# Fourth-quarter rows in a dead transform buffer, phase products in the spectrum buffers, and forward steps early in the inverse stage

## Chip, cores and metric

The kernel runs on one core of a Trainium2 chip. The metric is the device time of one execution in microseconds (us), median of several runs.

## The reference, cut to what matters

```python
# x: 8 x 5696 x 128 (batch, sequence, channels), h: 5696 x 128
Xf = np.fft.rfft(x, n=2 * S, axis=1); Hf = np.fft.rfft(h, n=2 * S, axis=0)
x  = np.fft.irfft(Xf * Hf[None], n=2 * S, axis=1)[:, :S]      # long convolution

theta = x @ w_theta                                            # 128 x 128
zr, zi = x * np.cos(theta), x * np.sin(theta)                  # the "phases"
y = einsum('ts,bsd->btd', w_tok_r, zr) + einsum('ts,bsd->btd', w_tok_i, zi)   # 5696 x 5696, twice
u = x + y
return u + np.maximum(u @ w_ch, 0.0)
```

## The kernel before

The kernel has three parts, one after the other.

1. **Block transform.** Eight groups (`bp`, `dh`: a batch pair and half of the channels). A group has forward steps A (tile `a`), spectrum steps B (products `u_t`, `v_t` of the spectrum with `hs`, which is loaded in chunks of 128 KB), inverse steps C (tile `g`) and output steps D (tile `yt`, stored to `yt_hbm`). C of one group is woven with A of the next; then B of the next is woven with D of this one. Stretches are named after the round of this loop: the "spectrum stretch of the seventh group" holds D of the seventh and B of the eighth group.
2. **Rows and phase steps.** The result, transposed by way of HBM, comes back as rows `ya0` and `ya1` (batches 0-3 and 4-7). 44 phase steps follow, 22 for each half: four transposes, a copy `y_ap`, its store, the matmuls of `theta`, three ACT operations (Abs, Sin, Sin), two DVE products, and the store of the products to `z_hbm`. Sixteen steps of the first half are woven into the last group.
3. **Block multiplication** (tiles `m`, `c`): a block scheme over the 5696 x 5696 weights. Its right-hand sides `b` are read back from `z_hbm` and summed ("`b` sums"), its weights `wb` are loaded, transposed and summed on DVE.

```python
fx = pool("fft_x", 1, xin)
fc = pool("fft_c", 1, conv, side="right")
fa = pool("fft_a", 1, conv, side="right")
fs = pool("fft_s", 2, conv, side="right")
fh = pool("fft_h", 4, conv, side="right")          # the hs buffers
...
# stage B, one chunk c
nc.scalar.activation(xs[:, :, :, :ck], ps, AF.Copy)
for r in range(2):
    nc.vector.tensor_tensor(uv[r][:, :, :, c0:c0 + ck], xs[:, :, :, :ck],
                            hv[:, r:r + 1, :, :ck].to_broadcast([P, 2, HD, ck]), op=mult)
load(c + LEAD)                                      # the hs load four chunks on, SP queue
...
# stage C, chunk q = 0, 8, ..., 120: 16 matmuls, then one eviction
if q % 24 == 16:
    nc.scalar.activation(...); nc.scalar.mul(...)   # on ACT
else:
    nc.vector.tensor_tensor(g_out, g_in, sg, op=mult)
...
# the phases
both = sb.tile([P, 2, n], F32, tag="both", name="both")       # pool "s2": 2 buffers
mag, red = both[:, 0, :], both[:, 1, :]
...
nc.scalar.activation(mag, r, AF.Abs)
nc.scalar.activation(red, r, AF.Sin, bias=zero_b[:m], scale=-TWO_PI)
nc.scalar.activation(mag, mag, AF.Sin, bias=half_pi[:m], scale=-TWO_PI)
zi = red.bitcast(BF16)[:, :n]                       # products in place
zr = mag.bitcast(BF16)[:, :n]
zi_eng.tensor_mul(zi, red, yflat)
nc.vector.tensor_mul(zr, mag, yflat)
nc.sync.dma_start(z_hbm[...], both[rows].bitcast(BF16)[:, :, :n])
...
def phase_step(ti, hh):
    ...
    y_ap = st["sby"].tile([P, 4, D], BF16, tag="y", name="y_ap")   # pool "s2y": 2 buffers
    nc.vector.tensor_copy(y_ap, tpz)
    nc.sync.dma_start(y2_hbm[ti]..., y_ap...)
...
for g, (bp, dh) in enumerate(groups):
    ...
    if dh == 0 and bp + 1 < B // 2:
        woven(c_, (a_ + [next_x], 0.7), now, load_)  # next_x loads 2.9 MB
    else:
        woven(c_, a_, now, load_)
    if g + 2 == len(groups):
        load_ya(0)                                  # 2.9 MB, ACT queue
    woven(b_, stage_d(st, bp, dh), now)
...
load_ya(1)                                          # after the last group
for step in steps0:
    step()
```

Of the kernel before, what the change touches and what calls it, by code (L numbers as in the profile page):

```python
# [10 lines left out]
F32 = mybir.dt.float32  # L11
BF16 = mybir.dt.bfloat16
F16 = mybir.dt.float16
# [9 lines left out]
def kernel(  # L23
# [10 lines left out]
    nc = tc.nc  # L34
    B, S, D = x.shape
    assert D == 128
    P = 128
# [29 lines left out]
    H = 22 * P  # L67
# [28 lines left out]
    def psum():  # L96
        return fp.tile([P, 2, 512], F32, tag="ps", name="ps")

    conv, setup, xin, pha = ExitStack(), ExitStack(), ExitStack(), ExitStack()

    def pool(name, bufs, stack, **kw):
        return stack.enter_context(tc.tile_pool(name=name, bufs=bufs, **kw))

    fx = pool("fft_x", 1, xin)
    fc = pool("fft_c", 1, conv, side="right")
    fa = pool("fft_a", 1, conv, side="right")
    fs = pool("fft_s", 2, conv, side="right")
    fh = pool("fft_h", 4, conv, side="right")
    s1 = pool("set_1", 1, setup, side="right")
    s2 = pool("set_2", 2, setup, side="right")  # L110

# [101 lines left out]

    def woven(*lists):

        lists = [l if isinstance(l, tuple) else (l, 1.0) for l in lists]
        steps = [((i + 0.5) / len(l) * w, n, f) for n, (l, w) in enumerate(lists) for i, f in enumerate(l)]
        for _, _, f in sorted(steps, key=lambda s: s[:2]):
            f()

# [88 lines left out]
    def stage_c(st):  # L309
        sg = sgn[:K1].unsqueeze(2).unsqueeze(1).to_broadcast([K1, 2, N2, 8])  # L310

        def chunk(q):
            if q == 0:
                st["g"] = fg.tile([P, 2 * N2, P], F16, tag="g", name="g_")
            ps = psum()
            for i in range(8):
                o = ps[:, i // 4, (i % 4) * P:(i % 4 + 1) * P]
                at = (q + i) * K1
                nc.tensor.matmul(o, u_t[:, at:at + P], r_u, start=True, stop=False)  # L319
                nc.tensor.matmul(o, v_t[:, at:at + P], r_v, start=False, stop=True)  # L320
            g_out = st["g"][:K1, :, q:q + 8].rearrange("p (r n) q -> p r n q", r=2)
            g_in = ps[:K1].rearrange("p a (q r n) -> p r n (a q)", q=4, r=2)
            if q % 24 == 16:
                nc.scalar.activation(g_out[:, :, :EN], g_in[:, :, :EN], AF.Copy)
                nc.scalar.mul(g_out[:, :, EN:], g_in[:, :, EN:], sgn[:K1, EN:EN + 1])
            else:
                nc.vector.tensor_tensor(g_out, g_in, sg, op=mult)
        return [lambda q=q: chunk(q) for q in range(0, 2 * HD, 8)]
# [39 lines left out]
    def phases_b(ti, y_ap, b0, nb, yT, sb, th_pool, th_tag, zi_eng, turns=None, tags=("red", "mag"), m=P,  # L368
# [2 lines left out]
        if theta_ps is None:  # L371
            theta_ps = th_pool.tile([P, n], F32, tag=th_tag, name="theta_ps")
        theta_ps = theta_ps[:m]
        if tags is None:
            both = sb.tile([P, 2, n], F32, tag="both", name="both")
            mag, red = both[:, 0, :], both[:, 1, :]
        else:
            red = sb.tile([P, n], F32, tag=tags[0], name="red")[:m]
            mag = sb.tile([P, n], F32, tag=tags[1], name="mag")[:m]
        y_ap = y_ap[:m]  # L380
        if turns is None:
            for b in range(nb):
# [21 lines left out]
        nc.scalar.activation(red, r, AF.Sin, bias=zero_b[:m], scale=-TWO_PI)  # L404
        nc.scalar.activation(mag, mag, AF.Sin, bias=half_pi[:m], scale=-TWO_PI)
        yflat = y_ap.rearrange("p b d -> p (b d)")
        zi = red.bitcast(BF16)[:, :n]
        zr = mag.bitcast(BF16)[:, :n]
        zi_eng.tensor_mul(zi, red, yflat)  # L409
        nc.vector.tensor_mul(zr, mag, yflat)  # L410
        cols = slice(b0 * D, b0 * D + n)
        for e in range((m + 63) // 64):
            rows = slice(e * 64, e * 64 + 64)
            if ti * P >= 2 * H:
                for r, z in enumerate((zr, zi)):
                    nc.sync.dma_start(zl_hbm[r, :, cols], z)
                continue
            p_, blk = divmod(2 * ti + e, 4 * NJ)
            i, j = divmod(blk, NJ)
            if tags is None:  # L420
                nc.sync.dma_start(z_hbm[:, p_, j, i, :, cols].rearrange("z t n -> t z n"),
                                  both[rows].bitcast(BF16)[:, :, :n])
            else:
                for r, z in enumerate((zr, zi)):
                    nc.sync.dma_start(z_hbm[r, p_, j, i, :, cols], z[rows])
# [20 lines left out]
        nc.scalar.mul(w_neg, w_theta_sb, -1.0)  # L446
        st["turns"] = (ones, plus, minus, w_neg)

    def load_ya(hh):
        st = sides["phases"]  # L450
        ya = st[hh] = pool(f"s2a{hh}", 1, pha, reuse_waits="tile").tile([P, 4, H], BF16, name=f"ya{hh}")
        PW = QR
        for p_ in range(4):
            nc.scalar.dma_start(ya[:, :, p_ * PW:p_ * PW + PW],
                                yt_hbm[:, 4 * hh:4 * hh + 4, p_ * PW:p_ * PW + PW])

    def phase_step(ti, hh):

# [18 lines left out]
    for g, (bp, dh) in enumerate(groups):  # L477
# [5 lines left out]
        if dh == 0 and bp + 1 < B // 2:  # L483
            def next_x(bp=bp):
                x16s[bp + 1] = load_x(bp + 1)
            woven(c_, (a_ + [next_x], 0.7), now, load_)
        else:
            woven(c_, a_, now, load_)
        if g + 2 == len(groups):
            xin.close()  # L490
            open_phases()
            load_ya(0)
        now = [steps0.pop(0) for _ in range(6)] if last else []
        woven(b_, stage_d(st, bp, dh), now)
    conv.close()

    CHUNKS = [(j0, min(CJ, NJ - j0)) for j0 in range(0, NJ, CJ)]
# [26 lines left out]
        nc.vector.tensor_add(b12, b11, b12)  # L524
        nc.vector.tensor_add(b21, b21, b22)  # L525

    load_ya(1)
    for step in steps0:
        step()
    early = iter(range(NE))  # L530
# [4 lines left out]
    for j in early:  # L535
        load_b(0, j, bpe)
    pha.close()
    psp.close()

    tp = ctx.enter_context(tc.tile_pool(name="tpool", bufs=5, reuse_waits="tile"))  # L540
# [354 lines left out]
```

## Time and profile before

The kernel took 2234.97 us (median of 3, 2234.55 to 2238.08; a fourth run, timed with the changed kernel, makes it 2235.14). To see where a change moves time, I cut the span at the first spectrum matmul of a group, the last spectrum matmul (in the round of the seventh group), the first and last output matmul of the last group, the Abs of the 23rd and of the 44th phase step, and the tenth addition to `c` (about the end of the multiplication's first tile pair). Each figure is the difference of the start times of two such instructions in the trace.

| stretch, us | before |
|---|---|
| setup, to the first spectrum matmul | 65.8 |
| transform, to the last spectrum matmul of the seventh group | 351.6 |
| last group's inverse stretch | 39.0 |
| last group's output stretch | 14.2 |
| to the 23rd phase step | 42.6 |
| 21 steps more, to the 44th | 67.2 |
| start of the multiplication | 56.4 |
| the rest | 1598.0 |

The chain of waits of the kernel before shows that the rest is PE at work on the tile `m`, which the change doesn't touch:

```profile
## 4 chain that ended last, share of the span: by engine, by line
PE 61%; DVE 5%; DMA 4%; POOL 2%; issue 1%; ACT 0%; DVEq 0%; ACTq 0%; SPq 0%; POOLq 0%
PE m L834 56%; DMA wb<-in_moe_w_tok_r_dram 2%; POOL wb L556 2%; DVE c L841 2%; DMA wb<-in_moe_w_tok_i_dram 1%; PE utp L646 1%; PE v L653 1%; DVE wt L565 1%; PE m L795 1%; PE m L797 1%; PE m L838 1%; PE tpz L595 0%; PE theta_ps L383 0%; DMA b<-z_hbm 0%; DVE b L525 0%
```

Next, the busy times of the engines by stretch, of the kernel before. The first number after the stretch is its length, and the last three are the granted clock of PE, the DMA share and GB/s. The rows are a set of inverse and forward steps, the spectrum and output steps after it, the coming of the second half of the rows, and the 22 steps of that half.

```profile
core 0: us, PE busy (x) PEld busy (x) DVE busy (x) ACT busy (x) POOL busy (x), PEclk, DMA share, GB/s
88.20:112.60 24.40, 24.37 (x316) 24.09 (x316) 12.63 (x11) 16.03 (x25) 4.23 (x8) 0.88 0.27 58
112.60:138.10 25.50, 17.17 (x491) 15.45 (x489) 15.81 (x25) 17.15 (x20) 4.19 (x8) 0.80 0.87 195
...
473.00:499.00 26.00, 10.63 (x66) 6.69 (x65) 7.14 (x13) 7.14 (x12) 11.52 (x22) 0.57 1.16 265
499.00:579.00 80.00, 48.21 (x326) 32.44 (x327) 52.54 (x92) 42.56 (x73) 0.00 (x0) 0.63 0.71 198
```

In the inverse and forward steps PE is busy all the time. In the spectrum and output steps no engine is: PE waits a third of it. In the phase steps no engine is busy for over two thirds of 80 us. The reasons stand in two lists of waits, again of the kernel before. First, what PE waited for before the first of the two inverse matmuls:

```profile
L319 PE MATMUL ps<-r_u,u_t x1024: 216/219/314, 88.2 to 454.3; 128*128 128x128 f16 x171
its engine sat idle before it (us, times) until:
  DVE u_t L303: 25.5, 8
```

PE stands still about 3 us at each of eight changes from spectrum to inverse steps, until the last products `u_t` are there. Second, the waits of the phase steps, from 440 to 580 us (engine, what it was about to do, what it waited for: us in all, times, longest):

```profile
ACT both L403 <- DMA z_hbm<-both: 38.2, 17, 4.6
...
PE ps L394 <- DVE y_ap L466: 20.4, 17, 2.6
...
ACT both L403 <- DMA ya<-yt_hbm: 9.3, 1, 9.3
...
DVE y_ap L466 <- DMA y_hbm<-y_ap: 5.0, 2, 3.6
```

ACT waits 38 us for stores of `both`: there are two such tiles, and ACT may not write a tile again before its products have landed in HBM.

### The profile page before, as it was taken

Reading aid. Unit: us, or ns where it says so; the run is one execution under the profiler, and the core shown is the slowest. Engines: PE = TensorE matmul, PEld = TensorE weight load, DVE = VectorE, ACT = ScalarE, POOL = GpSimd, SP = SyncE. Lnnn points to the kernel's source line nnn. Section 1 sums busy time; section 2 is a strip of 40 time slices with the busy share of each in tenths; the row PEclk is TensorE's granted clock in tenths of the full one; section 3 lists DMA queues with packets and bytes.
Section 4 is the critical chain, followed back from the end, with each engine's and each line's share of the span. In section 5 each row is a group of like instructions: output and inputs, shape, how many; then the busy total and the mean of one; then the engine's idle time right before and its main releaser. Section 6 shows DMA issues by size and latency. Waiting matters only on the chain.

```text
span 2234.9 us, 41331 instructions
## 1 busy us (share of the span) xinstructions
PE 2025.2 (91%) x15679; PEld 1134.5 (51%) x15679; DVE 1630.4 (73%) x2972; ACT 667.5 (30%) x1000; POOL 856.4 (38%) x1568
## 2 busy tenths in 40 slices
PE   3788888656699999999999997899999999999997
PEld 3777888644344444444444443344444444444443
DVE  7756656646798888877876766967777776867773
ACT  5767767655333232323320000011111111111111
POOL 4301010020145454455366552354444535454440
PEclk8688889876799999999999999899999999999998
DMA  7356463587899998989899989597878879797872
GB/s 142 78 129 161 123 158 85 157 208 209 235 172 171 174 177 167 173 143 171 163 191 149 152 128 279 101 154 135 153 135 139 148 130 154 129 159 128 152 130 53
DMA packets 410649, 340.39 MB, mean 152 GB/s; under 512 B 83288, under 2 KB 365784, under 8 KB 409336
## 3 DMA queue, kind: packets, MB, share of 16 engines
q0 software_dynamic: 221312, 143.00, 47.7%
q1 hardware_dynamic: 182032, 179.41, 27.9%
q10 hardware_dynamic: 7104, 15.34, 1.9%
q8 instruction: 123, 2.02, 0.4%
q14 instruction: 78, 0.63, 0.1%
HBM read 382.55 MB, written 97.93 MB: 215 GB/s over the span
## 4 chain that ended last, share of the span: by engine, by line
PE 61%; DVE 5%; DMA 4%; POOL 2%; issue 1%; ACT 0%; DVEq 0%; ACTq 0%; SPq 0%; POOLq 0%
PE m L834 56%; DMA wb<-in_moe_w_tok_r_dram 2%; POOL wb L556 2%; DVE c L841 2%; DMA wb<-in_moe_w_tok_i_dram 1%; PE utp L646 1%; PE v L653 1%; DVE wt L565 1%; PE m L795 1%; PE m L797 1%; PE m L838 1%; PE tpz L595 0%; PE theta_ps L383 0%; DMA b<-z_hbm 0%; DVE b L525 0%
## 5 line engine op out<-in xcount | busy, mean ns | idle before, releaser
L556 POOL DMA_DIRECT2D wb<-in_moe_w_tok_i_dram x720 | 387.8, 546 | 801.3 <-DVE wt L565 719.2
L556 POOL DMA_DIRECT2D wb<-in_moe_w_tok_r_dram x720 | 386.9, 548 | 283.4 <-ACT both L404 166.9
L834 PE MATMUL m<-b,wt 128*128 128x512 bf16 x1936 | 454.0, 382 | 22.2 <-DVE wt L565 21.2
L565 DVE STREAM_TRANSPOSE wt<-wb 128x384 f32<-128x384 f32 (+2 forms) x720 | 359.9, 524 | 124.5 <-PE m L834 69.2
L834 PEld LDWEIGHTS <-wt 128*128 128x128 bf16 x1936 | 189.7, 98 | 256.0 <-DVE wt L565 24.3
L841 DVE TENSOR_TENSOR c<-c,m 128x512 f32<-128x512 f32 x440 | 284.0, 671 | 0.0
L648 ACT ACTIVATE uts<-utp 128x512 bf16<-128x512 bf16 (+1 forms) x90 | 53.3, 593 | 616.1 <-PE utp L646 616.1
L319 PE MATMUL ps<-r_u,u_t 128*128 128x128 f16 x1024 | 139.9, 230 | 30.5 <-DVE u_t L303 25.5
L320 PE MATMUL ps<-r_v,v_t 128*128 128x128 f16 x1024 | 138.6, 230 | 0.0
L643 ACT ACTIVATE ub<-c 128x512 bf16<-128x512 f32 (+1 forms) x90 | 56.5, 628 | 227.5 <-DVE c L841 227.2
L319 PEld LDWEIGHTS <-u_t 128*128 128x128 f16 x1024 | 108.6, 106 | 26.9 <-DVE u_t L303 26.9
L127 POOL DMA_DIRECT2D x<-in_x_dram x64 | 34.1, 538 | 206.0 <-PE ps L190 195.9
L320 PEld LDWEIGHTS <-v_t 128*128 128x128 f16 x1024 | 106.6, 104 | 6.4 <-issue 5.7
L303 DVE TENSOR_TENSOR u_t<-xs,hs 128x1024 f16<-128x1024 f16 x96 | 64.9, 676 | 53.9 <-ACT xs L301 31.4
L301 ACT ACTIVATE xs<-ps 128x1024 f16<-128x1024 f32 x96 | 92.6, 990 | 21.9 <-PE ps L208 10.2
L208 PEld LDWEIGHTS <-w_t 64*128 64x128 f16 x3240 | 67.3, 106 | 52.8 <-issue 37.3
L190 PE MATMUL ps<-f_t,x 89*128 89x180 f16 x512 | 87.4, 308 | 3.5 <-ACT xs L301 2.3
L597 ACT ACTIVATE yb<-tpz 128x512 bf16<-128x512 bf16 (+1 forms) x46 | 27.5, 597 | 166.6 <-PE tpz L595 137.3
L190 PEld LDWEIGHTS <-x 89*128 89x128 f16 x512 | 74.4, 239 | 4.2 <-issue 3.9
L385 ACT ACTIVATE red<-theta_ps,magic 128x512 f32<-128x512 f32 (+1 forms) x46 | 31.6, 687 | 140.9 <-PE theta_ps L383 124.8
L655 DVE SCALAR_TENSOR_TENSOR c<-v,c 128x512 f32<-128x512 f32 (+1 forms) x90 | 61.5, 684 | 11.1 <-PE v L653 8.6
L409 DVE TENSOR_TENSOR both<-both,y_ap 128x512 bf16<-128x512 f32 x44 | 30.3, 689 | 48.6 <-ACT both L404 48.4
(2847 smaller groups left out, 3835.7 us busy)
## 6 DMA issues: line engine op xcount, KB each, us to landing
wb<-in_moe_w_tok_r_dram POOLq DMA_DIRECT2D x352, 96.0 KB, 4.7
wb<-in_moe_w_tok_i_dram POOLq DMA_DIRECT2D x352, 96.0 KB, 4.8
wb<-in_moe_w_tok_r_dram POOLq DMA_DIRECT2D x352, 80.0 KB, 4.5
wb<-in_moe_w_tok_i_dram POOLq DMA_DIRECT2D x352, 80.0 KB, 3.9
hs<-hf_hbm SPq DMA_DIRECT2D x192, 128.0 KB, 3.5
cp_hbm<-c SPq DMA_DIRECT2D x88, 256.0 KB, 2.2
c<-cp_hbm SPq DMA_DIRECT2D x88, 256.0 KB, 4.5
out_dram<-c SPq DMA_DIRECT2D x88, 256.0 KB, 4.4
```

Source lines behind the costliest of these rows:

```text
L190: nc.tensor.matmul(ps[:, i // 2, (i % 2) * 2 * K1:(i % 2 + 1) * 2 * K1], lhs(q + i), f1_t[:NB], start=True, stop=True)
L208: nc.tensor.matmul(ps[:, e, j * HD:(j + 1) * HD], w_t2[rows, c0 + j, N2 * (1 - ri):N2 * (3 - ri)], a_st["a"][rows, ri * K1 + c0 + j, :], s ...
L301: nc.scalar.activation(xs[:, :, :, :ck], ps, AF.Copy)
L303: nc.vector.tensor_tensor(uv[r][:, :, :, c0:c0 + ck], xs[:, :, :, :ck], hv[:, r:r + 1, :, :ck].to_broadcast([P, 2, HD, ck]), op=mult)
L319: nc.tensor.matmul(o, u_t[:, at:at + P], r_u, start=True, stop=False)
L320: nc.tensor.matmul(o, v_t[:, at:at + P], r_v, start=False, stop=True)
L556: nc.gpsimd.dma_start(wb[32 * i:32 * i + 32, :ng, :nj * 64], bass.AP(tensor=a.tensor, offset=a.offset + row0 * S + p * H + i * QR + j0 * 6 ...
L565: nc.vector.transpose(wt.rearrange("p j t r -> p (j t r)").bitcast(F32).rearrange("p (j g t) -> p g j t", j=TJ, g=4)[:, :ng, :nj], wb[:, : ...
L643: nc.scalar.activation(ub[:m].rearrange("p b d -> p (b d)"), c[:m], AF.Copy)
L655: nc.vector.scalar_tensor_tensor(c[:m], v[:m], 0.0, c[:m], op0=ALU.max, op1=ALU.add)
L834: nc.tensor.matmul(ms[q], a[q][:, j, :, r], bts[jj][q][:, r, :], start=(jj == 0 and r == 0), stop=(jj == NJ - 1 and r == 1 and q not in left))
L841: nc.vector.tensor_tensor(c, z, ms[q], op=op)
```

## The change

Its intent: `ya1` is loaded early, into the place of the transform's dead tile `a`, and its last quarter (channels 64-127 of batches 6 and 7) is copied from `yt` in SBUF instead of going through HBM; the phase products go to the four `hs` buffers, dead by then, so that ACT's tiles are free after the multiply; forward steps stand earlier in the inverse stage, three chunks of them before its first chunk, where PE waited. Row loads go from ACT's queue to SP's, and ACT evicts other inverse chunks than before.

```diff
+    fa = pool("fft_a", 1, xa)
+    fh = pool("fft_h", 4, xa)
     fx = pool("fft_x", 1, xin)
     fc = pool("fft_c", 1, conv, side="right")
-    fa = pool("fft_a", 1, conv, side="right")
     fs = pool("fft_s", 2, conv, side="right")
-    fh = pool("fft_h", 4, conv, side="right")
 ... (woven now takes a start and an end for each list)
-            if q % 24 == 16:
+            if q >= 64 and q % 16 == 0:
 ...
-            both = sb.tile([P, 2, n], F32, tag="both", name="both")
-            mag, red = both[:, 0, :], both[:, 1, :]
+        red = sb.tile([P, n], F32, tag=(tags or ("red", "mag"))[0], name="red")[:m]
+        mag = sb.tile([P, n], F32, tag=(tags or ("red", "mag"))[1], name="mag")[:m]
 ...
+            zz = fh.tile([P, 2, HD * CK], F16, tag="hs", name="zz").bitcast(BF16)[:, :, :n]
+            zr, zi = zz[:, 0], zz[:, 1]
 ...
-                                  both[rows].bitcast(BF16)[:, :, :n])
+                                  zz[rows])
 ...
+    def load_ya1(yt=None):
+        st = sides["phases"]
+        if yt is None:
+            a_ = fa.tile([P, 2 * K1, HD], F16, tag="a", name="ya1")
+            ya = st[1] = a_...                        # 4 batches x H rows
+            for p_ in range(2):
+                nc.sync.dma_start(ya[:, :2, ...], yt_hbm[:, 4:6, ...])
+            nc.sync.dma_start(ya[:HD, 2:], yt_hbm[:HD, 6:8, :H])
+        else:
+            for e in range(2):
+                nc.sync.dma_start(st[1][HD:, 2 + e, :],
+                                  yt[64 * e:64 * e + 64].rearrange("p m n -> p (m n)")[:, :H])
 ...
-            woven(c_, (a_ + [next_x], 0.7), now, load_)
-        else:
-            woven(c_, a_, now, load_)
+            a_ = a_ + [next_x]
+        woven((c_, 0.06 if a_ else 0.0, 1.0), (a_, 0.0, 0.55), now, load_)
         if g + 2 == len(groups):
             xin.close()
             open_phases()
-            load_ya(0)
+            load_ya0()
         now = [steps0.pop(0) for _ in range(6)] if last else []
-        woven(b_, stage_d(st, bp, dh), now)
+        woven(b_, (stage_d(st, bp, dh), 0.0, 1.1 if b_ else 1.0), now)
+        if g + 2 == len(groups):
+            load_ya1()
+    load_ya1(st["yt"])
```

More of the change, by code (lines that the diff above doesn't have):

```diff
@@ L97, in psum @@
         return fp.tile([P, 2, 512], F32, tag="ps", name="ps")
-    conv, setup, xin, pha = ExitStack(), ExitStack(), ExitStack(), ExitStack()
+    conv, setup, xa, xin, pha = (ExitStack() for _ in range(5))
     def pool(name, bufs, stack, **kw):
         return stack.enter_context(tc.tile_pool(name=name, bufs=bufs, **kw))
+    fa = pool("fft_a", 1, xa)
+    fh = pool("fft_h", 4, xa)
     fx = pool("fft_x", 1, xin)
     fc = pool("fft_c", 1, conv, side="right")
-    fa = pool("fft_a", 1, conv, side="right")
     fs = pool("fft_s", 2, conv, side="right")
-    fh = pool("fft_h", 4, conv, side="right")
     s1 = pool("set_1", 1, setup, side="right")
@@ L214, in woven @@
     def woven(*lists):
-        lists = [l if isinstance(l, tuple) else (l, 1.0) for l in lists]
-        steps = [((i + 0.5) / len(l) * w, n, f) for n, (l, w) in enumerate(lists) for i, f in enumerate(l)]
+        lists = [l if isinstance(l, tuple) else (l, 0.0, 1.0) for l in lists]
+        steps = [(w0 + (i + 0.5) / len(l) * (w1 - w0), n, f)
+                 for n, (l, w0, w1) in enumerate(lists) for i, f in enumerate(l)]
         for _, _, f in sorted(steps, key=lambda s: s[:2]):
@@ L373, in phases_b @@
         theta_ps = theta_ps[:m]
-        if tags is None:
-            both = sb.tile([P, 2, n], F32, tag="both", name="both")
-            mag, red = both[:, 0, :], both[:, 1, :]
-        else:
-            red = sb.tile([P, n], F32, tag=tags[0], name="red")[:m]
-            mag = sb.tile([P, n], F32, tag=tags[1], name="mag")[:m]
+        red = sb.tile([P, n], F32, tag=(tags or ("red", "mag"))[0], name="red")[:m]
+        mag = sb.tile([P, n], F32, tag=(tags or ("red", "mag"))[1], name="mag")[:m]
         y_ap = y_ap[:m]
@@ L406, in phases_b @@
         yflat = y_ap.rearrange("p b d -> p (b d)")
-        zi = red.bitcast(BF16)[:, :n]
-        zr = mag.bitcast(BF16)[:, :n]
+        if tags is None:
+            zz = fh.tile([P, 2, HD * CK], F16, tag="hs", name="zz").bitcast(BF16)[:, :, :n]
+            zr, zi = zz[:, 0], zz[:, 1]
+        else:
+            zi = red.bitcast(BF16)[:, :n]
+            zr = mag.bitcast(BF16)[:, :n]
         zi_eng.tensor_mul(zi, red, yflat)
@@ L447, in open_phases, with load_ya0 @@
         st["turns"] = (ones, plus, minus, w_neg)
-    def load_ya(hh):
-        st = sides["phases"]
-        ya = st[hh] = pool(f"s2a{hh}", 1, pha, reuse_waits="tile").tile([P, 4, H], BF16, name=f"ya{hh}")
-        PW = QR
-        for p_ in range(4):
-            nc.scalar.dma_start(ya[:, :, p_ * PW:p_ * PW + PW],
-                                yt_hbm[:, 4 * hh:4 * hh + 4, p_ * PW:p_ * PW + PW])
+    def load_ya0():
+        ya = sides["phases"][0] = pool("s2a", 1, pha, reuse_waits="tile").tile([P, 4, H], BF16, name="ya0")
+        for p_ in range(4):
+            nc.sync.dma_start(ya[:, :, p_ * QR:p_ * QR + QR], yt_hbm[:, 0:4, p_ * QR:p_ * QR + QR])
+    def load_ya1(yt=None):
+        st = sides["phases"]
+        if yt is None:
+            a_ = fa.tile([P, 2 * K1, HD], F16, tag="a", name="ya1")
+            ya = st[1] = a_.rearrange("p k d -> p (k d)")[:, :4 * H].bitcast(BF16).rearrange(
+                "p (b t) -> p b t", b=4)
+            for p_ in range(2):
+                nc.sync.dma_start(ya[:, :2, p_ * 2 * QR:(p_ + 1) * 2 * QR],
+                                  yt_hbm[:, 4:6, p_ * 2 * QR:(p_ + 1) * 2 * QR])
+            nc.sync.dma_start(ya[:HD, 2:], yt_hbm[:HD, 6:8, :H])
+        else:
+            for e in range(2):
+                nc.sync.dma_start(st[1][HD:, 2 + e, :],
+                                  yt[64 * e:64 * e + 64].rearrange("p m n -> p (m n)")[:, :H])
     def phase_step(ti, hh):
@@ L485, in next_x @@
                 x16s[bp + 1] = load_x(bp + 1)
-            woven(c_, (a_ + [next_x], 0.7), now, load_)
-        else:
-            woven(c_, a_, now, load_)
+            a_ = a_ + [next_x]
+        woven((c_, 0.06 if a_ else 0.0, 1.0), (a_, 0.0, 0.55), now, load_)
         if g + 2 == len(groups):
@@ L525, in sum_b @@
         nc.vector.tensor_add(b21, b21, b22)
-    load_ya(1)
     for step in steps0:
@@ L537 @@
     pha.close()
+    xa.close()
     psp.close()
```

## The prediction

> **What bounds the kernel now.** Of 2235 us, the chain of waits gives 56% to the block multiplication (tile `m`), steady from about 637 us and untouched by the change; the stretch to gain in is 88-637 us. Busy time per stretch there:
> - Four even transform groups: 24-26 us of forward/inverse steps (PE busy 24), then 25.5 us of spectrum/output steps (PE busy 17). Odd groups: 25 + 18 us. The difference is spectrum loads (`hs`) behind the 2.9 MB load of the next `x` (200 GB/s, until 128 us in the first group), or in the seventh group behind the phase rows (`ya`).
> - At each change from spectrum to inverse steps PE waits 2.4 to 4.7 us for the last spectrum product, 21 us in seven groups; the granted clock is then 0.5 for 7-14 us. The Trainium skill (TensorE: Matmul & The Clock Gate, Part 1) says that the clock is halved after an idle window of about 3.4 us; the trace's clock steps are multiples of 3.4 us, which agrees.
> - 473-499 us: the second half of the rows goes to HBM and back; ACT waits 9.3 us at once for it; DMA share 1.16.
> - 499-579 us: 22 phase steps, 3.6 us each, though ACT needs 1.7-1.9 and DVE 1.6. ACT waits 38 us in all for `z_hbm<-both`: two buffers are held until their stores land.
> - 579-637 us: DVE-bound start of the multiplication (53 of 58 us).
>
> **What the change does.**
> 1. Three forward chunks (0.5 us warm, about double cold) stand before the first inverse chunk and fill the wait; one output chunk moves behind the last spectrum chunk. 2-2.5 us in seven groups: 16 us.
> 2. The forward steps end after 9 of 16 inverse chunks, not 11 (even) or 16 (odd). The next `x` starts 1.5 us earlier (three times), the rows 6 us ahead of the spectrum loads that they delayed (once): 4 + 5 us. Fewer half-clock windows: 5 us.
> 3. `ya1` is loaded early into the dead `a` buffer, its last quarter copied from SBUF: 2.9 MB leave the 473-499 stretch.
> 4. Products go to the four `hs` buffers, so ACT's tiles come free after the multiply, not the store. Steps fall to 2.2-2.8 us, not 1.8: one stores 384 KB, and stretches of step stores alone move about 200 GB/s, 1.9 us a step (an estimate from these two), with 4 MB of `b` loads besides. The Trainium skill (Trainium Kernel Development and Optimization, Key Constraints) says that all queues share 16 DMA engines; their share is 0.7-1.2 here, which agrees.
> 5. By the instruction order two instead of four `b` sums stand among the phase steps; the others (3 us each on DVE) fall into the DVE-bound start: +6 us.
>
> **Sum.** Transform 30 us, last group's phases 3, rows and phase steps 25 (from 106 to about 80), later start -6 to -8: 50 us, all on the critical path, as the multiplication starts earlier by it. Predicted 2185 us, 8 in 10 between 2162 and 2208. Faster by over 2% (under 2190.3) 0.58, within 2% 0.40, slower 0.02.
>
> **What would show it.** The first inverse matmul's wait for `u_t` falls from 21 us to under 8; spectrum/output stretches of even groups fall from 25.5 to 23, the seventh's to about 20; ACT doesn't wait for `ya`, and under 10 us for `z_hbm` stores; phase steps take 2.5 us; the multiplication is steady near 587 us, its 35 us a tile pair unchanged.
>
> **What would make it wrong.** DMA saturates and phase steps stay near 3 us; the last group's stores wait in the in-order queue behind the `ya1` load, which itself waits for the transform's output to land; `b` and weights arrive late. The gain is larger if the transform keeps full clock.

## The result, and the profile after

The changed kernel took 2214.99 us (median of 4, 2211.21 to 2218.57) against 2235.14 (median of 4) of the kernel before. The ratio is 0.9907, with a 95% interval of 0.9888 to 0.9926: about 20 us faster, within 2%, and some 30 us short of the prediction. A ratio is the mean time of one kernel's fast runs over that of the other's of the same rounds, so it is not quite the ratio of the medians quoted. The same pair gave 0.9931 (run `r_after`, below). It was run at another time.

| stretch, us | before | predicted change | after | measured change |
|---|---|---|---|---|
| setup | 65.8 | 0 | 65.8 | 0 |
| transform | 351.6 | -30 | 331.7 | -19.9 |
| last inverse + output stretch | 53.2 | -3 | 61.1 | +7.9 |
| to 23rd and 44th step | 109.8 | -25 | 89.6 | -20.2 |
| start of the multiplication | 56.4 | +6 to +8 | 67.7 | +11.3 |
| the rest | 1598.0 | 0 | 1596.3 | -1.7 |

The chain of waits after:

```profile
## 4 chain that ended last, share of the span: by engine, by line
PE 63%; DVE 3%; DMA 3%; POOL 2%; issue 1%; ACT 0%; DVEq 0%; SPq 0%; ACTq 0%; POOLq 0%
PE m L850 58%; DMA wb<-in_moe_w_tok_r_dram 2%; POOL wb L572 1%; DVE c L857 1%; DMA wb<-in_moe_w_tok_i_dram 1%; PE v L669 1%; PE utp L662 1%; PE m L811 1%; PE m L813 1%; PE m L854 1%; DVE wt L581 1%; PE tpz L611 0%; PE theta_ps L380 0%; POOL wl L630 0%; DMA z_hbm<-mag 0%
```

The stretches that answer to those shown of before, with the last group's inverse stretch added (third row, 47 us; 39 before):

```profile
core 0: us, PE busy (x) PEld busy (x) DVE busy (x) ACT busy (x) POOL busy (x), PEclk, DMA share, GB/s
88.80:112.20 23.40, 23.40 (x310) 23.09 (x312) 14.34 (x12) 15.09 (x22) 5.30 (x10) 0.88 0.35 75
112.20:132.80 20.60, 15.06 (x485) 13.78 (x485) 13.61 (x21) 15.07 (x18) 3.15 (x6) 0.83 0.85 193
397.50:444.50 47.00, 33.78 (x413) 28.84 (x413) 33.44 (x49) 24.75 (x43) 0.00 (x0) 0.85 0.61 164
...
490.00:547.00 57.00, 32.40 (x295) 22.48 (x294) 42.09 (x75) 37.47 (x64) 0.00 (x0) 0.88 0.77 196
```

PE's wait for the last product before the first inverse matmul has fallen as wanted. The prediction spoke of the first seven changes, without the last group, in which no forward steps are left: there the wait fell from 20.9 to 6.2 us, under the 8 predicted. All eight changes:

```profile
L320 PE MATMUL ps<-r_u,u_t x1024: 216/219/314, 88.8 to 442.0; 128*128 128x128 f16 x171
its engine sat idle before it (us, times) until:
  DVE u_t L304: 10.1, 6
```

The waits of the last group and the phase steps after, from 398 to 548 us:

```profile
ACT mag L400 <- PE ps L397: 49.1, 21, 12.1
PEld L393 <- issue: 35.5, 37, 4.9
PE ps L391 <- DVE y_ap L480: 28.8, 23, 4.7
DVE zz L410 <- ACT red L401: 20.3, 23, 4.2
DVE y_ap L480 <- DMA y_hbm<-y_ap: 17.7, 6, 9.0
...
ACT g__8351 L325 <- PE ps L321: 11.0, 1, 11.0
...
PE ps L478 <- DMA ya<-yt: 6.4, 2, 5.2
```

ACT waits for neither product stores nor rows any more. In their place the copy `y_ap` waits 17.7 us for stores of the tile `y_ap`, PE waits for that copy, and ACT for PE. Read this chain backwards: ACT waits for PE (49.1), PE for `y_ap` (28.8, of which the 23 copies themselves, at 0.42 us, are about 10), `y_ap` for a store (17.7). And the rows are not free either: PE waits 6.4 us for their last quarter, the copies from `yt`. A wait named after an engine is often another's wait handed on.

### The profile page after: what moved, and what is told of

The parts are those of the page before. It is cut to its first block, busy times and chain, and to the rows that moved or that the text cites. A ratio compares the mean times of both kernels' runs of the same rounds, so it can differ in the third digit from the quotient of the medians.

```text
span 2212.3 us, 41297 instructions
## 1 busy us (share of the span) xinstructions
PE 2015.5 (91%) x15679; PEld 1123.8 (51%) x15679; DVE 1648.3 (75%) x2980; ACT 671.6 (30%) x984; POOL 859.6 (39%) x1568
## 4 chain that ended last, share of the span: by engine, by line
PE 63%; DVE 3%; DMA 3%; POOL 2%; issue 1%; ACT 0%; DVEq 0%; SPq 0%; ACTq 0%; POOLq 0%
PE m L850 58%; DMA wb<-in_moe_w_tok_r_dram 2%; POOL wb L572 1%; DVE c L857 1%; DMA wb<-in_moe_w_tok_i_dram 1%; PE v L669 1%; PE utp L662 1%; PE m L811 1%; PE m L813 1%; PE m L854 1%; DVE wt L581 1%; PE tpz L611 0%; PE theta_ps L380 0%; POOL wl L630 0%; DMA z_hbm<-mag 0%
## 5 line engine op out<-in xcount | busy, mean ns | idle before, releaser
L320 PE MATMUL ps<-r_u,u_t 128*128 128x128 f16 x1024 | 137.3, 231 | 16.3 <-DVE u_t L304 10.1
L320 PEld LDWEIGHTS <-u_t 128*128 128x128 f16 x1024 | 108.1, 106 | 13.8 <-DVE u_t L304 13.8
L127 POOL DMA_DIRECT2D x<-in_x_dram x64 | 34.2, 540 | 197.2 <-PE ps L190 186.8
L304 DVE TENSOR_TENSOR u_t<-xs,hs 128x1024 f16<-128x1024 f16 x96 | 69.8, 727 | 36.8 <-ACT xs L302 21.6
L208 PEld LDWEIGHTS <-w_t 64*128 64x128 f16 x3240 | 63.8, 105 | 41.7 <-issue 27.1
L304 DVE TENSOR_TENSOR v_t<-xs,hs 128x1024 f16<-128x1024 f16 x96 | 67.6, 704 | 0.0
```

What stands on the lines that cost most here:

```text
L208: nc.tensor.matmul(ps[:, e, j * HD:(j + 1) * HD], w_t2[rows, c0 + j, N2 * (1 - ri):N2 * (3 - ri)], a_st["a"][rows, ri * K1 + c0 + j, :], s ...
L320: nc.tensor.matmul(o, u_t[:, at:at + P], r_u, start=True, stop=False)
```

## The experiments

All but `e11` are edits of the changed kernel. Every kernel was timed in 3 rounds. All outputs are right. The changed kernel itself ran only beside e5 to e7 (`r_after`); the others are compared with it by their ratios to the kernel before, and by their traces. The theories, as they are named in the expectations: **A**, the forward chunks placed ahead of the inverse stage (the "lead") are worth far less than the 16 us predicted. **B**, the last inverse stretch grows because row loads stand in SP's queue ahead of the stores of the phase steps, and one of them waits for `yt_hbm` to land. **C**, the copies from SBUF come too late behind other transfers. **D**, the `hs` buffers for the products are the change's main gain. **E**, the late start comes from where the `b` tiles lie. **F**, the two `y_ap` buffers are the next limit.

The stretches of all runs, from one trace each (us):

| run | setup | transform | last inverse | last output | to 23rd step | to 44th | start | rest |
|---|---|---|---|---|---|---|---|---|
| before | 65.8 | 351.6 | 39.0 | 14.2 | 42.6 | 67.2 | 56.4 | 1598.0 |
| after | 65.8 | 331.7 | 46.9 | 14.2 | 33.7 | 55.9 | 67.7 | 1596.3 |
| r_after | 63.8 | 334.2 | 45.6 | 14.6 | 34.2 | 57.9 | 67.5 | 1599.0 |
| e1_no_lead | 63.9 | 338.3 | 44.6 | 14.1 | 34.2 | 56.9 | 67.3 | 1597.5 |
| e2_rows_pool | 66.2 | 336.0 | 45.0 | 12.8 | 34.2 | 58.3 | 67.7 | 1596.2 |
| e3_copy_first | 66.0 | 333.9 | 47.0 | 15.6 | 34.1 | 62.5 | 63.5 | 1597.5 |
| e4_held_tiles | 63.5 | 335.6 | 48.3 | 15.1 | 40.8 | 65.9 | 66.7 | 1597.3 |
| e5_b_place | 65.8 | 335.0 | 44.6 | 14.6 | 34.2 | 60.2 | 69.3 | 1597.9 |
| e6_last_row_pool | 65.8 | 332.2 | 40.5 | 13.8 | 34.7 | 59.3 | 67.0 | 1595.3 |
| e7_yap4 | 64.0 | 335.5 | 38.7 | 13.8 | 30.1 | 49.3 | 68.7 | 1599.5 |
| e8_yap4_row_pool | 63.6 | 337.9 | 40.3 | 13.3 | 29.1 | 50.0 | 69.4 | 1595.0 |
| e9_yap6_row_pool | 65.7 | 331.3 | 40.4 | 13.3 | 24.4 | 45.5 | 74.3 | 1596.5 |
| e10_old_weave | 63.6 | 348.8 | 45.8 | 14.6 | 34.5 | 57.2 | 67.9 | 1599.5 |
| e11_before_yap4 | 63.4 | 348.9 | 38.8 | 16.5 | 44.9 | 71.4 | 50.5 | 1596.8 |

How far single traces differ by chance is seen in the transform column: ten kernels with the same transform order (all but before, e1, e10 and e11) give 331.3 to 337.9, mean 334.3. A difference of 3 us in one trace shows nothing.

### r_after: the changed kernel again

No edit. It gives a second comparison and the base for e5 to e7.

> The changed kernel once more, unaltered, so that the next three are compared with it on the same chip. All theories: ratio to before 0.988 to 0.993, as recorded (0.9907); the stretch from the last phase step to the end of the first tile pair 66-69 us again (56 before the change), the last group's inverse stretch 46-47 us (39 before).

Measured: 2216.05 us against 2231.08, ratio 0.9931 (0.9914 to 0.9947). The two comparisons of the change with before give 20 us (the first) and 15 us (this one).

### e1_no_lead: one forward chunk ahead of the inverse stage, not three

```diff
-        woven((c_, 0.06 if a_ else 0.0, 1.0), (a_, 0.0, 0.55), now, load_)
+        woven((c_, 0.0, 1.0), (a_, 0.0, 0.55), now, load_)
```

> The changed kernel (2215 us) with the inverse chunks starting at position 0.0 again, so that no three forward chunks stand ahead of the first inverse chunk; all else as changed. Theory A (the lead fills the wait but pays it back: the three chunks run at half clock and slow the last spectrum products on DVE): first inverse matmul's wait for u_t goes from 10 back to about 20 us, but forward/inverse stretches get shorter by nearly as much, total +2 to +6 us, 2217 to 2221. Rival, the prediction's step 1 (the lead is worth 2-2.5 us in each of seven groups): +14 to +16 us, 2229 to 2231.

The trace shows that this takes away only two of the three chunks: four forward matmuls, one chunk, still stand before the first inverse matmul in seven groups. (In the kernel before and in e10 that is so in three of the seven, those that reload `x`, and in the others none.)

Measured: 2219.75 us against 2230.81, ratio 0.9946 (0.9926 to 0.9967). The transform took 338.3 us, 4.0 more than the mean of the ten with the lead. Against the other ratios of the changed transform (0.9907, 0.9931) the two chunks are worth 3 to 9 us, with overlapping intervals. Theory A holds: not 16 us.

Why so little? PE's wait did shrink, but the inverse stage did not begin sooner for it. Over the seven changes of stage, by the starts and ends of matmuls in the traces (us):

| | before | e10 | e1 | after | r_after |
|---|---|---|---|---|---|
| last spectrum to first inverse matmul | 25.4 | 28.9 | 30.0 | 34.3 | 34.8 |
| first to last inverse matmul | 167.8 | 169.0 | 165.6 | 159.6 | 159.7 |
| sum | 193.2 | 197.9 | 195.6 | 193.9 | 194.5 |

What the inverse stretches gave up, the handover took. (A part of its growth, 3.5 us, is there in e10 too, which has the old order of forward steps but one output chunk behind the last spectrum chunk, as the changed kernel has.) All that the transform gained lies in the spectrum stretches, which are the matter of e10.

Does the clock play a part? Here are 3.4 us windows around the first change of stage, of the kernel before; its inverse steps start at 137.9:

```profile
135.10:138.50 3.40, 0.70 (x14) 0.40 (x12) 2.99 (x6) 1.45 (x3) 0.00 (x0) 1.00 0.71 190
138.50:141.90 3.40, 3.40 (x31) 3.40 (x32) 1.22 (x1) 0.77 (x1) 0.00 (x0) 0.50 0.98 221
```

And the same change of stage in the changed kernel, where the lead runs from 133.0 to 135.5 and the first inverse matmul stands at 136.5:

```profile
132.10:135.50 3.40, 2.82 (x58) 2.53 (x52) 2.72 (x4) 3.40 (x5) 0.00 (x0) 1.00 0.49 145
135.50:138.90 3.40, 2.41 (x20) 2.22 (x21) 1.53 (x5) 1.80 (x3) 0.00 (x0) 0.51 1.06 250
138.90:142.30 3.40, 3.40 (x31) 3.40 (x30) 2.39 (x2) 1.60 (x3) 0.00 (x0) 0.50 0.90 233
```

Before, PE was busy 0.70 of 3.40 us in the window of the wait, and one window at half clock followed (0.50). After, the lead raised that to 2.82 of 3.40, and *two* windows at half clock followed. So filling the wait did not keep the clock up here. But this is one change of stage, and the others differ: over the seven inverse stretches PE had half clock for 31.5 us before, 33.2 in e1, 32.1 after and 31.2 in `r_after`. The clock is not what ate the gain. The Trainium skill (TensorE: Matmul & The Clock Gate, Part 1) says that the clock falls to half after an idle window of about 3.4 us. The length of the windows agrees, but here a window in which PE was busy 83% by the profile was followed by half clock too.

The handover grew because the last spectrum products come later: from the last spectrum matmul to the end of the last product it is 27.8 us before, 33.0 in e1 and 37.7 after, summed over the seven changes. Of that, 1.7, 3.7 and 10.1 us are what the last products take beyond their usual length (0.69 us, and 0.39 for the last, smaller pair). These are the full-size products `u_t` in the transform, of the kernels before, after, e1_no_lead and e10_old_weave, in this order (mean ns of one after the busy us; then the idle time before them and what ended it):

```profile
L303 DVE TENSOR_TENSOR u_t<-xs,hs 128x1024 f16<-128x1024 f16 x86 | 60.4, 702 | 52.4 <-ACT xs L301 31.0 <-DMA hs<-hf_hbm 20.1 <-ACT yt L345 0.5
```

```profile
L304 DVE TENSOR_TENSOR u_t<-xs,hs 128x1024 f16<-128x1024 f16 x86 | 65.3, 760 | 35.7 <-ACT xs L302 21.6 <-DMA hs<-hf_hbm 13.4
```

```profile
L304 DVE TENSOR_TENSOR u_t<-xs,hs 128x1024 f16<-128x1024 f16 x86 | 60.8, 707 | 41.9 <-ACT xs L302 26.9 <-DMA hs<-hf_hbm 13.2 <-ACT yt L346 0.9
```

```profile
L304 DVE TENSOR_TENSOR u_t<-xs,hs 128x1024 f16<-128x1024 f16 x86 | 60.2, 700 | 50.2 <-ACT xs L302 30.3 <-DMA hs<-hf_hbm 18.8
```

In these three kernels without the full lead one takes 700 to 707 ns on the mean; in the ten with it, 735 to 767. A few slow ones make the difference. In the first change of stage of the changed kernel (start, length in us):

```profile
132.39 1.03 DVE L304 TENSOR_TENSOR v_t<-xs,hs 128x1024 f16<-128x1024 f16 x1
132.97 0.72 PE L190 MATMUL ps<-f_t,x 89*128 89x180 f16 x4
134.10 1.43 DVE L304 TENSOR_TENSOR u_t<-xs,hs 128x1024 f16<-128x1024 f16 x1 [0.68 <-ACT xs L302]
134.12 1.34 PE L190 MATMUL ps<-f_t,x 89*128 89x180 f16 x8 [0.43 <-ACT xs L302]
134.97 2.33 ACT L197 ACTIVATE a__2336<-ps 128x720 f16<-128x720 f32 x3
```

Two products took 1.03 and 1.43 us instead of 0.69, just ahead of the inverse stage, which waits for them. Beside both run the forward *matmuls*; ACT's evictions of forward chunks start only after the first. The full-size products (`u_t` and `v_t`) of the whole transform agree. Of 176 in the changed kernel, 149 with neither beside them took 0.69 us on the mean, 11 beside forward matmuls alone 1.10, 10 beside both 1.07, and 3 beside evictions alone 0.68 (three more met either for under 0.1 us); in e1, 8 beside the matmuls alone took 0.97 and 10 beside the evictions alone 0.69. In all ten kernels with the lead, every product over 0.85 us (14 to 18 a trace) has a forward matmul beside it. So the slowing comes with the lead (e1) and goes with PE's forward matmuls, not with ACT's evictions; what the two engines meet at is not shown.

### e10_old_weave: the old places of the forward steps

```diff
-        woven((c_, 0.06 if a_ else 0.0, 1.0), (a_, 0.0, 0.55), now, load_)
+        woven(c_, (a_, 0.0, 0.7 if dh == 0 and bp + 1 < B // 2 else 1.0), now, load_)
```

> The changed kernel with the old weaving of forward and inverse chunks (no lead, forward chunks over the whole stage, or 0.7 of it where x is reloaded); output chunks stay as changed. Beside e1 (no lead alone: spectrum matmuls of the seventh group end at 402 us against 398 to 401 in the kernels with the lead) it shows what ending the forward steps early is worth. The prediction's step 2 (next x 1.5 us earlier three times, phase rows 6 us ahead once, 9 us in all, and fewer half-clock windows): that end moves to 410 to 414 us, the seventh spectrum stretch from 17 back to 20-23 us, total 8 to 12 us over e1, 16 over the changed kernel. Rival (the early forward steps only move work within a stage that PE bounds anyway): under 4 us over e1, at 402 to 406 us.

Measured: 2229.35 us against 2233.85, ratio 0.9975 (0.9955 to 0.9996). By the ratios this is 6.5 us slower than e1 (on another chip, with overlapping intervals); by the traces the transform takes 348.8 us, 10.5 more than in e1 and about as long as in the kernel before with its 351.6 and 348.9 (before and e11). The ratios fall between the two expectations, the traces on the side of the early end. Its spectrum stretch of the seventh group takes 21.2 us instead of 16.6 to 17.5 in the ten kernels, and the products wait 18.8 us for `hs` loads instead of 13.4 (last two lines above). So nearly all of the transform's gain is in the order: by the traces some 10 us from the early end of the forward steps (with one forward chunk ahead in seven groups instead of three), some 4 from the other two chunks of the lead, and nothing to speak of from the other evictions or the later output steps.

### e2_rows_pool: the row loads on POOL's queue

```diff
-                nc.sync.dma_start(ya[:, :2, ...], yt_hbm[:, 4:6, ...])
+                nc.gpsimd.dma_start(ya[:, :2, ...], yt_hbm[:, 4:6, ...])
-            nc.sync.dma_start(ya[:HD, 2:], yt_hbm[:HD, 6:8, :H])
+            nc.gpsimd.dma_start(ya[:HD, 2:], yt_hbm[:HD, 6:8, :H])
```

> The changed kernel with the three early loads of the second row half (ya1) issued from POOL, which is idle there, instead of SP. Theory B (the third load waits for the transform's output to land and, in SP's in-order queue, holds back the y stores behind it, so that two y_ap buffers stall DVE, then ACT and PE): the last group's inverse stretch falls from 41 us to 32-34, ACT's 11 us idle at 412-423 us is gone, total 2205 to 2209. Rival (the 2.2 MB of rows saturate the DMA engines whichever queue issues them): the stretch stays at 39 us or more, total within 3 us of 2215.

Measured: 2217.84 us against 2230.81, ratio 0.9929 (0.9908 to 0.9951): no gain. But a loss hides a gain. From the first inverse to the first output matmul the last group fell from 41.8 to 35.6 us; the time before it grew by most of that (45.0 us in all, against 45.6 and 46.9), since the loads, free of SP's order, now ran ahead of the last `hs` loads, and DVE waited 5.7 us for those. This run moved two things at once. e6 moves one.

### e6_last_row_pool: only the load that waits

```diff
-            nc.sync.dma_start(ya[:HD, 2:], yt_hbm[:HD, 6:8, :H])
+            nc.gpsimd.dma_start(ya[:HD, 2:], yt_hbm[:HD, 6:8, :H])
```

> The changed kernel with only the third early load of the rows (the one that waits for the transform's output to land) issued from POOL; the first two stay on SP behind the spectrum loads. In e2 all three were on POOL, the inverse stretch itself fell from 41.8 to about 35.6 us from its first to its last matmul, but the two unblocked loads ran ahead of the last spectrum loads and delayed them by 5 us. Theory B: without that, the stretch from the last spectrum matmul to the first output matmul falls from 46.9 to 39-42 us and total is 4 to 8 us less than the changed kernel. Rival (DMA bandwidth): no more than 2 us less.

Measured: 2210.94 us against 2231.08, ratio 0.9911 (0.9896 to 0.9926), 5 us less than `r_after` on the same chip, with an inverse stretch of 40.5 us instead of 45.6. The two intervals overlap a little, but all four runs of e6 lie below all four of `r_after`, and the stretch agrees with the time. Theory B holds. In the changed kernel SP's queue stood still in order, as the waits of SP show:

```profile
SPq L465 <- DMA yt_hbm<-yt: 5.1, 1, 5.1
```

For 5.1 us SP waited for the seventh group's output to land before it could issue this load. The stores of `y_ap` and of the products that were issued behind it waited with it, and the two `y_ap` buffers with them. The Trainium skill (DMA: Bandwidth & Descriptors, section "Issuing engines are not separate DMA queues") says that issuing from several engines saves only the issue time on the sequencer, usually small. That is not what was won here: the issue of this load took 0.63 us, and 5 us came from not waiting in line.

### e3_copy_first: the SBUF copies ahead of the last stores

```diff
+                if (bp, dh) == groups[-1]:
+                    load_ya1(yt)                    # in stage D, ahead of the yt_hbm stores
...
-    load_ya1(st["yt"])
```

> The changed kernel with the two SBUF copies of the last quarter of the rows issued before the two 712 KB stores of the transform's output, not after them. Theory C (the copies land after 12 us because they stand behind the 1.4 MB in the same queue): copies land in 5-7 us, ACT's idle of 12 us at 473-485 us falls to 6 or less, the second 22 phase steps start 5-7 us earlier, total 2208 to 2211. Rival (the stretch is at a DMA share of 0.99 with 2.2 MB of weight loads beside it; order doesn't matter as the bytes are the same, and the y stores only wait longer): total within 2 us of 2215.

Measured: 2218.2 us against 2230.81, ratio 0.9936 (0.9915 to 0.9956): no gain. The copies landed in 7.7 us (median) instead of 12.3, and PE's wait for them fell from 6.4 to 0.6 us; but DVE still waited for the stores of `y_ap`, as the waits of DVE in this run show:

```profile
DVE y_ap L482 <- DMA y_hbm<-y_ap: 15.9, 5, 8.5
```

Theory C falls: the copies were late, but weren't the last thing waited for. The steps even grew, to 62.5 us, and the start of the multiplication shrank by about as much (63.5 us).

### e4_held_tiles: the products in place again

```diff
+        if tags is None:
+            both = sb.tile([P, 2, n], F32, tag="both", name="both")
+            mag, red = both[:, 0, :], both[:, 1, :]
...
-            zz = fh.tile([P, 2, HD * CK], F16, tag="hs", name="zz").bitcast(BF16)[:, :, :n]
-            zr, zi = zz[:, 0], zz[:, 1]
+        zi = red.bitcast(BF16)[:, :n]
+        zr = mag.bitcast(BF16)[:, :n]
```

> The changed kernel with the phase products written in place into ACT's own tiles again and stored from there (two tile pairs held until their stores land), all else as changed. Theory D (the held tiles cost most of the phase steps' time): the 22 steps from 485 us take 76-81 us again instead of 65, of which the start of the multiplication gives back a part, total +6 to +12, 2221 to 2227. Rival (the steps are bound by the stores' 200 GB/s, not by the held tiles): the 22 steps stay under 70 us, total within 3 us of 2215.

Measured: 2234.8 us against 2230.81, ratio 1.001 (0.9993 to 1.0027). Theory D holds, and the loss is larger than the 6 to 12 us expected: without the `hs` buffers for the products, nothing is left of the gain. The two phase-step stretches grow by 17 us (106.7 against 89.6), and ACT waits for stores as it did before:

```profile
ACT both L404 <- DMA z_hbm<-both: 46.2, 25, 4.3
```

The transform's gain (16 us) is still there, and is given back in the last group (+10 us against before) and at the start of the multiplication (+10 us).

### e5_b_place: the `b` tiles over memory that is free earlier

```diff
+    placed = {}
...
-    with tc.tile_pool(name="bpool", bufs=1, reuse_waits="tile") as bp, \
-         tc.tile_pool(name="cpool", bufs=1, reuse_waits="tile") as cp, \
+    with tc.tile_pool(name="cpool", bufs=1, reuse_waits="tile") as cp, \
+         tc.tile_pool(name="bpool", bufs=1, reuse_waits="tile") as bp, \
...
+            if p == 0:
+                for j in (NJ - 1, *range(NE, NJ - 1)):
+                    placed[p, j] = bp.tile([P, 7 * 1024], BF16, tag=f"b{j}", name=f"b{j}")
```

In the changed kernel the tiles `b4` and `b5` lie over `ya1` and the products' buffers, so their loads start only 5 to 7 us after the last step.

> The changed kernel with the multiplication's pools placed so that b4 to b9 no longer lie over the forward buffer, the product buffers and ACT's tiles of the phase steps (the small output tiles and b10 lie there instead). Theory E (the new layout puts b4 and b5 over buffers that are released by the very last phase step and its stores, so that the in-order queues start the last 7 MB of b loads 7 us later against the last step than before): b loads start within 3 us of the last step instead of 7, the stretch from the last step to the end of the first tile pair falls from 67.7 to 58-62 us, total 5 to 9 us less than the changed kernel. Rival (the prediction's step 5: the stretch is longer because two more sums stand behind the steps on DVE, 6 us, and because faster steps leave more to load): at most 2 us less.

Measured: 2222.53 us against 2231.08, ratio 0.9968 (0.995 to 0.9986). Theory E falls: the first of these loads started within 3 us of the last step, the start took 69.3 us instead of 67.5, and the kernel was slower. The last of the loads landed hardly sooner, though (29.8 us after the last step instead of 31.7; 24.9 in the kernel before), so what an earlier *end* of the loads would give was not tested.

### e7_yap4: four `y_ap` buffers

```diff
-        sby = pool("s2y", 2, pha, reuse_waits="tile")
+        sby = pool("s2y", 4, pha, reuse_waits="tile")
```

> The changed kernel with four instead of two y_ap buffers. Theory F (in the last group and between the transform's end and the second half of the steps, DVE waits for stores of y out of two buffers, 17.7 us in all, once the product buffers no longer hold the steps): the waits of the y copy for y stores fall under 6 us, the last group's inverse stretch to 40-43 us, the 33.7 us from the last output matmul to the 23rd step to 28-31, total 6 to 12 us less than the changed kernel. Rival (these stretches are bound by DMA, which moves the same bytes): the waits move to the product buffers' stores, total within 2 us.

Measured: 2198.86 us against 2231.08, ratio 0.9854 (0.9835 to 0.9873), 17 us less than `r_after` on the same chip and more than the 6 to 12 expected. Theory F holds, and not its rival, DMA bandwidth: the same bytes are moved. The copies' waits, in the changed kernel and then in e7:

```profile
its engine sat idle before it (us, times) until:
  DMA y_hbm<-y_ap: 17.7, 6
```

```profile
  DMA y_hbm<-y_ap: 3.4, 2
```

The last inverse stretch is 38.7 us, as before the change, and the two step stretches fall from 92.1 (`r_after`) to 79.4 us, 2.35 us a step.

### e11_before_yap4: four `y_ap` buffers in the kernel before

The same edit in the kernel before.

> The kernel before the change with four y_ap buffers and nothing else. Theory F says that buffers bind one after the other: there ACT's two tile pairs, held until their stores land, bind first (ACT waited 38 us for them), y stores only 5 us, so that four y_ap buffers give at most 3 us: ratio 0.998 to 1.000, phase steps 3.2 us as before. Rival (y_ap binds by itself, and e7's 17 us would have been had without the change): ratio 0.993 or less.

Measured: 2235.29 us against 2233.85, ratio 1.0007 (0.9988 to 1.0025): nothing. There `both` binds, and ACT waits 55.5 us for its stores. The two limits lie in series: `y_ap` alone is worth nothing, the product buffers about 18 to 23 us (the ratio of e4 against those of the changed kernel), and `y_ap` after them 17 us more. That it is `both`, and no other part of the change, that hides `y_ap` is read from this wait; e4 with four `y_ap` buffers was not run.

### e8_yap4_row_pool and e9_yap6_row_pool: the parts together

e8 is e6 and e7 together; e9 has six `y_ap` buffers.

```diff
-        sby = pool("s2y", 2, pha, reuse_waits="tile")
+        sby = pool("s2y", 6, pha, reuse_waits="tile")    # 4 in e8
-            nc.sync.dma_start(ya[:HD, 2:], yt_hbm[:HD, 6:8, :H])
+            nc.gpsimd.dma_start(ya[:HD, 2:], yt_hbm[:HD, 6:8, :H])
```

> The changed kernel with four y_ap buffers and with the one early row load that waits for the transform's output issued from POOL: e6 and e7 together. e7 alone was 17 us faster than the changed kernel of the same rounds, e6 alone 4 to 5 us. Theory F (the two y_ap buffers are what binds, and the blocked queue matters only because they are so few): with four buffers the blocked queue is ridden out, so that the two together give at most 3 us more than e7, ratio 0.984 to 0.986. Rival (two separate costs): gains add up, ratio about 0.983 or less, the last group's inverse stretch 36 us or less against 38.7 in e7.

> As e8 with six y_ap buffers. Theory F: with four the wait for y stores is 3.4 us in all, so two more give under 2 us; then the four product buffers and the DMA rate bind: the phase steps stay at 2.3 us. Rival (stores are still late by more than four steps where the weight loads run): the 30 us between the last output matmul and the 23rd step fall to 26 or less, total 3 to 5 us less than e8.

Measured on one chip, against 2233.85: e8 2198.79 us, ratio 0.984 (0.9821 to 0.9858), and e9 2194.25 us, ratio 0.9824 (0.9805 to 0.9843). The gains of e6 and e7 don't add: e8 is no faster than e7 (0.984 and 0.9854), which fits with four buffers being enough to bridge the wait of SP's queue. Six buffers take 9 us off the step stretches (69.9 against 79.1), and 5 us come back at the start of the multiplication (74.3 against 69.4), where DVE now makes 50 `b` sums. So the expectation of e9 failed and its rival was right: the stretch to the 23rd step fell to 24.4 us ("26 or less"), a step to 2.17 us (not 2.3), so stores of `y_ap` were still late with four buffers. Of the time itself, e9 against e8 gives 3.6 us by the ratios, with overlapping intervals. e9 is the fastest kernel: 1.8% under the kernel before, and, by the ratios to it on different chips, 0.8 to 1.1% under the changed one.

## Why the prediction was wrong

The predicted time was 2185 us and the likeliest class "faster by over 2%"; measured were 2215 us, and 0.7 to 0.9% faster in the two comparisons. Step by step:

- **What bounds the kernel: right.** The rest of the multiplication was not changed (1598.0 and 1596.3 us), and everything gained or lost ahead of it shows in the span.
- **Step 1, "three forward chunks ... fill the wait ... 2-2.5 us in seven groups: 16 us": the step that failed most.** The wait was filled (20.9 to 6.2 us in the seven groups), but the prediction took the length of the wait for the gain. The handover from the last spectrum to the first inverse matmul grew from 25.4 to 34.3 us, the inverse stretches shrank by 8.2, and the sum stayed (193.2 and 193.9 us). What it left out is that the work put into the wait slows what is waited for: products with forward matmuls beside them take about 1.1 us instead of 0.69. By e1, two of the three chunks are worth about 4 us (3 to 9 by the ratios); the first chunk alone was not tested.
- **Step 2, the early end of the forward steps: right in kind, and in size for its first half.** Predicted were 4 + 5 us from loads, and about 10 us is what e10 against e1 shows in the traces (6.5 by the ratios). The half-clock time of the transform did fall, from 103 to 83 us (94 in e11, 80 in `r_after`; mean clock 0.85 to 0.87), but not under the inverse steps, and the "5 us" for it cannot be seen as a further gain. In all, the transform gave 15 to 20 us of 30.
- **Step 3, `ya1` early: right in what it removes, wrong in what it brings.** ACT no longer waits 9.3 us for rows, but PE waits 6.4 us for the copies from `yt`. And the last group, predicted 3 us shorter, took 8 longer. The prediction named the cause among its dangers ("the last group's stores wait in the in-order queue behind the `ya1` load") and gave it no time. It cost 5 us with two `y_ap` buffers (e6) and nothing with four (e8).
- **Step 4, products in the `hs` buffers: right, and large.** The 21 step intervals fell from 3.2 to 2.66 us, inside "2.2-2.8", and e4 shows that the change is worth nothing without it. Twenty of 25 us came. What the prediction overlooked is the next limit: `y_ap` has two buffers that are held until *their* store lands, just as `both` had. In the kernel before that cost 5.8 us of DVE's time and looked harmless; after, 17.7. Taking it away gives 17 us (e7): 8 in the last group and 13 in the steps, less some 3 elsewhere. As only 11 and 5 us were missing there, it accounts for about 13 of the 28 us missing (the 5 us of step 3 among them); the rest of its gain goes beyond the prediction. That 2.66 us fell inside the range is in part luck: the prediction set the range by the rate at which DMA moves the stores, but with the same stores and more `y_ap` buffers a step took 2.35 us (e7) and 2.17 (e9).
- **Step 5, the later start: right in kind, under-sized.** Predicted +6 to +8, measured +11.3. In the start stretch DVE makes 45 `b` sums instead of 35 (9 instead of 7 on each of five lines, at 0.68 us: 6.8 us), as predicted. DVE's waits in this stretch are 9.9 us instead of 6.4: 4.5 for the weights and 4.8 for PE (tile `m`) are new, and those for `b` and for ACT are gone but for 0.6. The new waits are not explained: neither an earlier start of the `b` loads (e5) nor slower steps (e4, 66.7 us) took the longer start away. That the weights are late because the last `b` loads (16 of 512 KB after the last step) run at the same time is argued, not shown, and stays open.

Added up by stretch, from the two traces: the transform 10 us short, the last group 11, the steps 5, the start 4, less 2 in the rest. That is 28 of 50 us, which leaves the 22.6 us by which the spans differ (2234.9 and 2212.3).

## What to carry to other kernels

When tiles are held until their stores land, count *every* tile of the step that is stored, not only the one that shows the largest wait: the second is hidden while the first binds, and shows its cost only once the first is gone (nothing in e11, 17 us in e7). A DMA that had to wait here held up what was issued behind it on the same engine for 5.1 us, so a load that depends on a late store belongs on a queue where nothing urgent follows, or behind enough buffers (e8). And work put into an engine's wait is worth the wait only if it doesn't slow what is being waited for: look at when the next stage begins, not at the wait.

## What the Trainium skill lacked or had wrong

- **TensorE: Matmul & The Clock Gate, Part 1** names an idle window of about 3.4 us as the cause of half clock. Here a window with PE busy 2.82 of 3.40 us by the profile was followed by half clock (0.51), as was one with 0.70 of 3.40 (0.50). In the transform of the changed kernel the clock fell to half 13 times, after windows with PE busy 0.22 to 0.82 of the time, while other windows from 0.65 up kept it. How much work in a window keeps the clock, traces don't settle. The windows' length agrees.
- **SBUF — State Buffer, section "Who interferes with whom"** says that only the port pair shared by VectorE and GpSimd causes contention. Here spectrum products on DVE took 1.03 and 1.43 us instead of 0.69 while PE ran forward matmuls and POOL had no instruction in the trace; in the transform of the changed kernel the 11 products beside forward matmuls alone took 1.10 us on the mean, the 149 without them 0.69. The cause may lie elsewhere than in SBUF's ports.
- **DMA: Bandwidth & Descriptors, section "Issuing engines are not separate DMA queues"** says, as does Trainium Kernel Development and Optimization, section "Key Constraints", that issuing from several engines saves only the time of issue. Here one load moved to another engine's queue took 5 us off (2216.05 to 2210.94 us), because it had held up stores behind it for 5.1 us while it waited.
- **No page that I read** says how long a small store takes to land beside other transfers, and so how long a tile is held by it. In the kernel before a product's store of 128 KB landed in 2.5 us (median) from 520 to 540 us and in 6.2 us from 473 to 499 us, where the rows and weights were loaded beside it, and with two buffers such stores, not any engine's work, set the length of a step (3.2 us).
